# Attention scores in four 32-row strips of the array, values after every key tile, keys split late

## The chip, the cores and the metric

The kernel runs on one core of one Trainium2 chip. The metric is the device time of one execution in microseconds; the time before is the median of three runs, 962.56 us (960.89 to 963.39).

## The reference

The input is one sequence of S = 2048 tokens of width D = 448. Attention with 16 heads of 28 and one shared key and value head is mixed, by a gate per token, with a token-shift MLP:

```python
g = sigmoid((x * gate_w).sum(-1, keepdims=True))
# A: grouped attention, H = 16, Dh = 28, one k and one v for all heads
q = (x @ wq).reshape(B, S, H, Dh).transpose(0, 2, 1, 3)
k, v = x @ wk, x @ wv
scores = einsum("bhqd,bkd->bhqk", q, k) * Dh ** -0.5
a = einsum("bhqk,bkd->bhqd", softmax(scores), v) ... @ wo
# B: layernorm, w1, gelu, four shifted quarters, w2, residual, then an MLP of 1792
h = gelu(layernorm(x) @ w1)
x1 = x + concat(shift(h quarters by +1, -1, +2, -2)) @ w2
b = x1 + gelu(layernorm(x1) @ w3) @ w4
out = g * a + (1 - g) * b
```

All inputs and outputs are fp32.

## The kernel before

Operands that need more precision than one fp32r matmul gives are split into a high part (a rounded copy) and a low part (the rest), and a product is the sum of three: high x high, low x high, high x low.

The kernel writes its instruction order by hand for all engines (`manual_schedule`), so each engine runs its instructions in the order in which the program issues them; waits come from the data. There are three stages.

1. Projections and token shift. `stage_q` projects q, and in spare columns k, v and the gate, for each of the four blocks of 512 tokens and each of four groups of heads, and writes them to DRAM (`qd`). `stage_kv` reads the rows of k back three times into `kf` (rows 0, 32 and 64) and those of v into `vT`, on the SP queue. `split_k` on POOL makes `kS` of it: high keys in rows 0 to 31 and 32 to 63, low keys in rows 64 to 95, ones in rows 96 to 127. It is called for block 0 before `stage_w1(2)`, for block 1 after `stage_w2(1)`, for block 2 after `stage_w1(3)` and for block 3 after `stage_w2(2)`. `kf` has two buffers. `stage_w2(3)` has the splits of the first w3 and w4 chunks between its tiles (`weights`), and these raise a memset of the padded rows on POOL (`split_w_high`, L110) and further loads on SP (`load_w34`, L548 and L549).
2. The MLP, by token block b and by chunk f of 128 of the 1792 columns: `w3_part` (11 matmuls, L134 to L138), two Gelu activations on ACT into `gh` and `gf` (L625, L626), the low part `gl` on DVE (L627), then `w4_part` two chunks later (12 matmuls, L635 to L637). The w3 products alternate between two banks (`mm_tile`).
3. Attention, in 16 units u: a block of 512 queries by a group of four heads. Scores are keys by queries, for 16 key tiles kt of 128 keys and four heads j. The queries of a unit stand in `qs`: high, low and high rows below one another (`q_rows`, three copies of rows on SP a unit), and two rows with the negative maximum, high and low. So one matmul of 98 rows gives all three split products and subtracts the maximum:

```python
nc.tensor.matmul(ps, kS[0:98, kt * P:(kt + 1) * P], q_of[u][0:98, j, :], start=True, stop=True)
```

ACT takes the exponential (L860), and `pv_group` multiplies it with the values and a column of ones, the four heads of a key tile in four column strips of 32 of the array, fp32 (two instructions each). The scores use seven PSUM banks in turn (`bank`); the value sums have one of their own. `VISITS` says after which key tiles PE goes to the values, and for how many of them:

```python
VISITS = {0: (-2, 0), 2: (0, 2), 4: (2, 4), 6: (4, 6), 8: (6, 8), 11: (8, 11), 14: (11, 14)}
```

Seven visits a unit take two or three tiles each. Between the scores, `pump` puts single matmuls of the output projection (`wo_job`, L769 to L773) or, in unit 0, of the last MLP chunk (`w4_job`, L798 to L802), and `max_part` (L210, one 256-column matmul for 64 keys) makes an estimate of the next unit's maxima, which `max_end` sends to rows 96 and 97 of `qs` in four small transfers. After a unit, `sums_begin` copies the value sums (L735), `recip` and `norm` divide (L753), and POOL splits the result (L756, L757) for `wo_job`. If a sum ever grows past a limit, a second pass (`redo`) with exact maxima follows at the end; it is not taken with these inputs.

Of the kernel before, what the change touches and what calls it, by code (L numbers as in the profile page):

```python
# [16 lines left out]
P = 128  # L17
# [24 lines left out]
def gated_mix_kernel(  # L42
# [25 lines left out]
    identR = keep.tile([P, P], F32R, name="identR")  # L68
    nc.vector.tensor_copy(identR, ident)
    x1 = keep.tile([P, NT, D], F32, name="x1")  # L70
    kS = keep.tile([P, S], F32R, name="kS")
# [14 lines left out]
    nc.gpsimd.memset(f32(kS)[96:128, :], 1.0)  # L86
# [53 lines left out]
    def stats_tile(pool, b, t, mv):  # L140
        st = pool.tile([P, 6], F32, tag="st", bufs=4, name=f"st_{pool.name}_{b}_{t}")
        nc.vector.bn_stats(st, x1[:, 4 * b + t, :])
        nc.vector.bn_aggr(mv[:, t, :], st)
# [35 lines left out]
    qs_of = [None, None]  # L179

    def q_load(u, raw):
        b, g = divmod(u, NG)
        qr_of[u] = raw
        nc.sync.dma_start(raw[0:4 * DH], qd[g, 0:4 * DH, 512 * b:512 * b + 512])

    def q_split(u, qh, ql):
        qr = qr_of.pop(u)[0:4 * DH]
        qh_of[u], ql_of[u] = qh[0:4 * DH], ql[0:4 * DH]
        nc.vector.tensor_copy(qh_of[u], qr)
        nc.vector.tensor_sub(ql_of[u], qr, f32(qh_of[u]))  # L190

    def q_rows(u):
        q_of[u] = qs_of[u % 2]
        for r, part in enumerate((qh_of[u], ql_of[u], qh_of[u])):
            nc.sync.dma_start(f32(q_of[u])[32 * r:32 * r + DH], f32(part))

    NU = NB * NG
    q_of = {}
# [7 lines left out]
    def max_part(u, t, tile_of):  # L206
        if t == 0:
            mx_of[u] = late.tile([P, 4, 4], F32, tag="mr", bufs=2, name=f"mr_{u}")
        ps = tile_of(f"m_{u}_{t}")[:, 0:4 * MK].rearrange("p (j k) -> p j k", j=4)
        nc.tensor.matmul(ps, qh_of[u][:, t * P:(t + 1) * P], khd[0:4 * DH], start=True, stop=True)  # L210
        nc.vector.reduce_max(mx_of[u][:, :, t], ps, axis=AX.X)  # L211

    def max_full(u, tile_of):
        mr = late.tile([P, 4, 4], F32, tag="mr", bufs=2, name=f"mf_{u}")
        for j in range(4):
            for t in range(4):
                mk = late.tile([P, NB], F32, tag="mk", bufs=2, name=f"mk_{u}_{j}_{t}")
                for kb in range(NB):
                    ps = tile_of(f"mf_{u}_{j}_{t}_{kb}")
                    nc.tensor.matmul(ps, q_of[u][0:96, j, t * P:(t + 1) * P], kS[0:96, kb * 512:kb * 512 + 512],  # L220
                                     start=True, stop=True)
                    nc.vector.reduce_max(mk[:, kb:kb + 1], ps, axis=AX.X)
                nc.vector.reduce_max(mr[:, j, t:t + 1], mk, axis=AX.X)
        mx_of[u] = mr

    def max_end(u):
        mr = mx_of.pop(u).rearrange("p j t -> p (j t)")
        mc = late.tile([P, 32], F32R, tag="mc", bufs=2, name=f"mc_{u}")
# [3 lines left out]
        mrow = late.tile([P, 32], F32, tag="mrow", bufs=2, name=f"mrow_{u}")  # L232
        nc.vector.transpose(mrow, f32(mc))
        for p in range(4):
            nc.sync.dma_start(f32(qs_of[u % 2])[96:98, :, :].rearrange("k j (t p q) -> k p (j t) q", p=4, q=32)[:, p],
                              mrow[32 * p:32 * p + 32, :])
# [4 lines left out]
    with tc.tile_pool(name="s1b", bufs=1) as s1b, \  # L241
# [77 lines left out]
        kf_of = {}  # L319

        def stage_kv(b):
            cols = slice(512 * b, 512 * b + 512)
            kf = s1b.tile([96, 512], F32, tag="kf", bufs=2, name=f"kf_{b}")
            for r in range(3):
                for g in range(2):
                    nc.sync.dma_start(kf[32 * r + 16 * g:32 * r + 16 * g + 16, :], qd[g, 4 * DH:P, cols])
            for g in range(2):
                nc.sync.dma_start(vT[32 * b + 16 * g:32 * b + 16 * g + 16, :], qd[2 + g, 4 * DH:P, cols])
            kf_of[b] = kf

        def split_k(b):
            cols = slice(512 * b, 512 * b + 512)
            kf = kf_of[b]
            nc.gpsimd.tensor_copy(kS[0:96, cols], kf)
            nc.gpsimd.tensor_tensor(kS[64:96, cols], kf[64:96, :], f32(kS)[64:96, cols], ALU.subtract)
# [172 lines left out]
        split_k(0)  # L508
# [10 lines left out]
        split_k(1)  # L519
# [3 lines left out]
        split_k(2)  # L523
# [3 lines left out]
        late = ctx.enter_context(tc.tile_pool(name="late", bufs=1, side="right", reuse_waits="tile"))  # L527
        khd = late.tile([P, 4, MK], F32R, name="khd")
        qh0 = late.tile([P, 512], F32R, tag="qh0", bufs=1, name="qh0")
        qs_of[0] = late.tile([P, 4, 512], F32R, name="qs0")  # L530
# [70 lines left out]
    with tc.tile_pool(name="s2", bufs=1, reuse_waits="tile") as s2, \  # L601
# [12 lines left out]
        def w3_part(b, f):  # L614
# [3 lines left out]
            if (b, f) == (NB - 1, NF - 1):  # L618
                gh = late.tile([P, 512], F32R, tag="qh0", bufs=1, name="gh_late")
# [4 lines left out]
            gf = s2.tile([P, 512], F32, tag="gf", bufs=2, name=f"gf_{b}_{f}")  # L624
# [14 lines left out]
        for b in range(NB):  # L639
            acc = [ps2.tile([P, 512], F32, tag="acc", bufs=4, name=f"acc_{b}_{t}") for t in range(4)]  # L640
            gs = {}
            for f in range(NF):
# [24 lines left out]
                if b == 1 and f == 1:  # L667
                    for z in (khd, qs_of[0][0:96]):
                        nc.gpsimd.memset(f32(z), 0.0)
                    for j in range(4):  # L670
                        nc.sync.dma_start(f32(khd)[j:4 * DH:4, j, :], f32(kS)[0:DH, 0:MK])
                    q_load(0, s2a.tile([P, 512], F32, tag="xn", bufs=1, name="qr_0"))
                if b == 1 and f == 5:
                    q_split(0, qh0, s2.tile([P, 512], F32R, tag="gl", bufs=3, name="ql_0"))
                    q_rows(0)
# [20 lines left out]
    with tc.tile_pool(name="s3", bufs=1, reuse_waits="tile") as s3, \  # L696
# [12 lines left out]
        qs_of[1] = s3.tile([P, 4, 512], F32R, name="qs1")  # L709
        nc.gpsimd.memset(f32(qs_of[1])[0:96], 0.0)  # L710
# [4 lines left out]
        def q_begin(u):  # L715
            q_split(u, s3.tile([P, 512], F32R, tag="qh", bufs=2, name=f"qh_{u}"),
                    s3.tile([P, 512], F32R, tag="ql", bufs=1, name=f"ql_{u}"))
# [3 lines left out]
        q_rows(1)  # L721
# [40 lines left out]
        def wo_job(u, t, end=None):  # L762
# [4 lines left out]
            held = banks.pop(0)  # L767
            ps = held[:, 0:D]
            nc.tensor.matmul(ps, onh[:, tok], woh[:, g, :], start=True, stop=False)  # L769
            yield  # L770
            nc.tensor.matmul(ps, onh[:, tok], wol[:, g, :], start=False, stop=False)  # L771
            yield
            nc.tensor.matmul(ps, onl[:, tok], woh[:, g, :], start=False, stop=True)  # L773
            banks.append(held)
# [17 lines left out]
        def w4_job(t):  # L792
# [3 lines left out]
            held = banks.pop(0)  # L796
            ps = held[:, 0:D]
            nc.tensor.matmul(ps, gh[:, tok], w4h[-1][:, 1, :], start=True, stop=False)  # L798
            yield
            nc.tensor.matmul(ps, gh[:, tok], w4l[-1][:, 1, :], start=False, stop=False)  # L800
            yield
            nc.tensor.matmul(ps, gl[:, tok], w4h[-1][:, 1, :], start=False, stop=True)  # L802
            banks.append(held)
            nc.vector.scalar_tensor_tensor(x1[:, n, :], ps, gi[:, n:n + 1], x1[:, n, :], op0=ALU.mult, op1=ALU.add)

        jobs = []
        current = [None]

        def pump():
            while current[0] or jobs:  # L810
                if not current[0]:
                    current[0] = jobs.pop(0)
                if next(current[0], True) is None:
                    return
                current[0] = None
                return
# [15 lines left out]
        WO_AT = (33, 36, 37, 40, 43, 44, 48, 50, 52, 53, 54, 55)  # L832
        M_AT = (5, 11, 17, 22)
        M_FIRST = (20, 29, 36, 40)
        W4_AT = (22, 29, 36, 37, 38, 41, 49, 50, 51, 54, 58, 61)
        WO_LAST = (36, 37, 38, 49, 50, 51)
        VISITS = {0: (-2, 0), 2: (0, 2), 4: (2, 4), 6: (4, 6), 8: (6, 8), 11: (8, 11), 14: (11, 14)}

        for k in range(NU * NT + 1):
            u, kt = divmod(k, NT)  # L840
            if k < NU * NT:
                if kt == 8 and 0 < u < NU - 1:
                    q_rows(u + 1)
# [3 lines left out]
                if kt == WO_AT[0] // 4 and u > 0:  # L847
                    for t in range(4):
                        jobs.append(wo_job(u - 1, t))
                if k == 0:  # L850
                    for t in range(4):
                        jobs.append(w4_job(t))
                pump_at = W4_AT if u == 0 else WO_AT if u < NU - 1 else WO_LAST
                p_of[k] = []
                for j in range(4):
                    n, at = 4 * k + j, 4 * kt + j
                    ps = bank(f"s_{n}")
                    nc.tensor.matmul(ps, kS[0:98, kt * P:(kt + 1) * P], q_of[u][0:98, j, :], start=True, stop=True)  # L858
                    p = s3.tile([P, 512], F32, tag="p", bufs=PB, name=f"p_{n}")
                    nc.scalar.activation(p, ps, AF.Exp, scale=SCALE)  # L860
                    p_of[k].append(p)
                    if at in pump_at:
                        pump()
                    if at == 12 and sums:
                        norms.append(recip(*sums.pop()))
                    if at == 27 and norms:
                        norm(*norms.pop())
                    m_at = M_AT if u else M_FIRST
                    if u + 1 < NU and at in m_at:
                        t = m_at.index(at)  # L870
                        max_part(u + 1, t, bank)
                        if t == 3:
                            max_end(u + 1)
            if k == NU * NT:
                while current[0] or jobs:
                    pump()
# [49 lines left out]
        def tail_wo(t):  # L926
            for _ in wo_job(u, t, end):
                pass
# [46 lines left out]
        with tc.If(again > 0, label="redo"):  # L975
            for b in range(NB):
                for g in range(NG):
# [3 lines left out]
                    q_rows(u)  # L981
# [3 lines left out]
                    for kt in range(NT):  # L985
                        for j in range(4):
                            ps = bank(f"s2_{u}_{kt}_{j}")
                            nc.tensor.matmul(ps, kS[0:98, kt * P:(kt + 1) * P], q_of[u][0:98, j, :],
                                             start=True, stop=True)
# [59 lines left out]
```

## Time and profile before

| | |
|---|---|
| runs | 960.89, 962.56, 963.39 us; median 962.56 |
| span of the profiled execution | 960.5 us (its own time is not given beside it) |
| PE busy | 950.6 us, 99% of the span |
| ACT busy | 648.1 us, 67% |
| stage 1, to the first w3 product | to 129.1 us |
| stage 3, first to last attention scores | 402.8 to 944.5 us |
| one unit in the middle of stage 3 | 34.0 us |

Engines are PE (matmul), PEld (weight loads, which overlap PE), DVE (VectorE), ACT (ScalarE), POOL (GpSimd) and SP (which here only issues DMAs). In a row of a group, "out<-in" names the tiles, then come the shapes and the count; behind the bar stand the busy time and the mean of one instruction in ns, and then the idle time of the engine in front of them with what ended it. Matmuls are pipelined, so the mean of one (some 0.4 us) is longer than the distance from one to the next. In a timeline a row is start, length, engine, line and operation, merged over neighbours of one kind; in the chain of waits it is start, length, engine, tile and line. The name of a tile stands without its number: the banks of stage 3 are all "bank".

### The profile page before, as it was taken

How to read it: one execution, taken by the hardware profiler on the slowest of the kernel's cores; microseconds unless marked ns; L12 is line 12 of the kernel's file. 1: busy time of each engine (PE TensorE's matmuls, PEld its weight loads, DVE VectorE, ACT ScalarE, POOL GpSimd, SP SyncE). 2: the span in 40 equal slices, each digit the busy share in tenths (PEclk: the TensorE clock that was granted, in tenths of full speed). 3: DMA queues.
4: the chain of work that ended last, by engine and by line, in shares of the span. 5: the costliest groups of instructions: out<-in, count | busy, mean ns of one | idle time of the engine just before them, and what ended most of it. 6: DMA issues, size and time to landing. Idle time of an engine off the chain costs nothing.

```text
span 960.5 us, 13540 instructions
## 1 busy us (share of the span) xinstructions
PE 950.6 (99%) x5203; PEld 633.0 (66%) x5203; DVE 286.4 (30%) x573; ACT 648.1 (67%) x1266; POOL 112.8 (12%) x136
## 2 busy tenths in 40 slices
PE   9999999999999999999999999999999999999997
PEld 6788888888888888754555555555555555545554
DVE  4664254533432421221222212222122222212112
ACT  5442444322322222499999999999999999999994
POOL 3243400200001420040000000000000000000000
PEclk9999999999999999999999999999999999999999
DMA  9812452111300300021011021011111101210101
GB/s 308 276 42 61 139 164 83 41 53 29 83 1 1 83 1 10 23 56 46 19 48 42 22 78 52 17 36 51 44 59 40 47 18 40 75 49 12 37 13 42
DMA packets 44439, 56.22 MB, mean 59 GB/s; under 512 B 9536, under 2 KB 27664, under 8 KB 44368
## 3 DMA queue, kind: packets, MB, share of 16 engines
q1 hardware_dynamic: 41344, 49.82, 17.7%
q10 hardware_dynamic: 3024, 5.47, 1.6%
q8 instruction: 42, 0.69, 0.3%
q14 instruction: 29, 0.24, 0.1%
HBM read 32.19 MB, written 11.67 MB: 46 GB/s over the span
## 4 chain that ended last, share of the span: by engine, by line
PE 96%; DMA 3%; DVE 0%; SPq 0%; issue 0%
PE bank L858 27%; PE pv L827 24%; PE acc L635 5%; PE acc L637 5%; PE acc L636 5%; PE g L135 4%; PE g L134 4%; PE g L136 4%; DMA w2raw<-in_w_dram 1%; PE hs L421 1%; PE hs L420 1%; PE hs L422 1%; PE bank L773 1%; PE bank L771 1%; PE bank L769 1%; PE g L137 1%
## 5 line engine op out<-in xcount | busy, mean ns | idle before, releaser
L860 ACT ACTIVATE p<-bank 128x512 f32<-128x512 f32 x1024 | 511.4, 642 | 34.3 <-PE bank L858 31.4
L858 PE MATMUL bank<-qs,kS 98*128 98x512 f32 x1024 | 306.0, 408 | 0.0
L858 PEld LDWEIGHTS bank<-qs,kS 98*128 98x128 f32 x1024 | 184.3, 188 | 134.0 <-issue 93.1
L827 PE MATMUL pv<-p,vext 128*32 128x512 f32 x2048 | 243.1, 598 | 0.0
L625 ACT ACTIVATE gh<-g 128x512 fp32r<-128x512 f32 x55 | 32.9, 598 | 182.5 <-PE g L138 182.5
L827 PEld LDWEIGHTS pv<-p,vext 128*32 128x32 f32 x2048 | 58.6, 109 | 116.3 <-issue 108.9
L627 DVE TENSOR_TENSOR gl<-gf,gh 128x512 fp32r<-128x512 f32 x55 | 38.3, 697 | 161.9 <-ACT gf L626 157.6
L635 PE MATMUL acc<-w4h,gh 128*128 128x448 f32 x220 | 79.9, 363 | 0.0
L637 PE MATMUL acc<-w4h,gl 128*128 128x448 f32 x220 | 79.9, 363 | 0.0
L636 PE MATMUL acc<-w4l,gh 128*128 128x448 f32 x220 | 79.7, 362 | 0.0
L781 DVE SCALAR_TENSOR_TENSOR ot<-bank,gg,ot 128x448 f32<-128x448 f32 x44 | 30.0, 684 | 143.3 <-ACT p L860 95.7
L135 PE MATMUL g<-al,w3h 128*128 128x512 f32 x168 | 65.6, 391 | 0.0
L134 PE MATMUL g<-ah,w3h 128*128 128x512 f32 x168 | 65.6, 391 | 0.0
L136 PE MATMUL g<-ah,w3l 128*128 128x512 f32 x168 | 65.6, 391 | 0.0
L756 POOL CAST onh<-on 128x512 fp32r<-128x512 f32 x15 | 9.1, 609 | 472.4 <-DVE on L753 472.4
L211 DVE TENSOR_REDUCE mr<-bank 128x4 f32<-128x256 f32 x60 | 25.6, 427 | 105.5 <-PE bank L210 104.4
L636 PEld LDWEIGHTS acc<-w4l,gh 128*128 128x128 f32 x220 | 41.3, 188 | 4.2
L635 PEld LDWEIGHTS acc<-w4h,gh 128*128 128x128 f32 x220 | 41.3, 188 | 4.1
L637 PEld LDWEIGHTS acc<-w4h,gl 128*128 128x128 f32 x220 | 41.3, 188 | 3.0
L735 DVE COPY o<-pv 128x512 f32<-128x512 f32 x15 | 10.4, 691 | 99.4 <-PE pv L827 99.4
L136 PEld LDWEIGHTS g<-ah,w3l 128*128 128x128 f32 x168 | 31.5, 188 | 6.8
L135 PEld LDWEIGHTS g<-al,w3h 128*128 128x128 f32 x168 | 31.5, 188 | 5.6
(195 smaller groups left out, 971.4 us busy)
## 6 DMA issues: line engine op xcount, KB each, us to landing
qs<-qh SPq DMA_DIRECT2D x32, 224.0 KB
qd<-qf ACTq DMA_DIRECT2D x16, 256.0 KB
rb<-rd SPq DMA_DIRECT2D x15, 256.0 KB
x<-in_x_dram SPq DMA_DIRECT2D x4, 896.0 KB
xd<-xt SPq DMA_DIRECT2D x16, 224.0 KB
w34raw<-in_w_dram SPq DMA_DIRECT2D x7, 512.0 KB
qr<-qd SPq DMA_DIRECT2D x16, 224.0 KB
qs<-ql SPq DMA_DIRECT2D x16, 224.0 KB
```

The source lines that it names most:

```text
L134: nc.tensor.matmul(ps, wh[:, c, :], ah[:, c, :], start=(c == 0), stop=False)
L135: nc.tensor.matmul(ps, wh[:, c, :], al[:, c, :], start=False, stop=False)
L136: nc.tensor.matmul(ps, wl[:, c, :], ah[:, c, :], start=False, stop=False)
L625: nc.scalar.activation(gh, ps, AF.Gelu_apprx_tanh)
L627: nc.vector.tensor_sub(gl, gf, f32(gh))
L635: nc.tensor.matmul(ps, gh[:, tok], w4h[i][:, k, :], start=(f == 0), stop=False)
L636: nc.tensor.matmul(ps, gh[:, tok], w4l[i][:, k, :], start=False, stop=False)
L637: nc.tensor.matmul(ps, gl[:, tok], w4h[i][:, k, :], start=False, stop=(f == stop))
L781: nc.vector.scalar_tensor_tensor(ot_of[n], ps, gg[:, n:n + 1], before, op0=ALU.mult, op1=ALU.add)
L827: nc.tensor.matmul(pv[32 * j:32 * j + 32, :], vext[:, kt, :], ps[j], start=(kt == 0), stop=(kt == NT - 1), tile_position=(0, 32 * j))
L858: nc.tensor.matmul(ps, kS[0:98, kt * P:(kt + 1) * P], q_of[u][0:98, j, :], start=True, stop=True)
L860: nc.scalar.activation(p, ps, AF.Exp, scale=SCALE)
```

## The change

Each head's scores are computed in one strip of 32 rows of the array. `kH` and `kL` hold the high and low keys four times, once in each strip of 32 partitions, with two rows of ones behind the 28 key rows; `qh` and `ql` of a unit hold head j in strip j as they come from DRAM, and the maxima go into rows 28 and 29 of each strip (eight small transfers a unit). A score is three matmuls of 30, 28 and 28 rows, issued in three rounds over the four heads, four banks at a time. `q_rows`, `qs` and its copies are gone. The values follow every key tile, two tiles behind the scores (`LAG`). A projection job is issued whole, after the scores of tiles 8, 10, 12 and 14, a maximum matmul after those of tiles 1, 3, 4 and 5. `kf` is one buffer of 128 partitions, filled by eight transfers a block (`load_k`); the splits of blocks 0 to 3 stand in and behind `stage_w2(2)`, and each load waits for the split before. Some pools get fewer buffers (`gf` one, not two), others more (`qh` and `ql` three).

```diff
+    def score(u, ps, j, keys, first=None, i=None):
+        r = 32 * j
+        for n, (rows, w, a) in enumerate(((first or DH + 2, kH, qh_of[u]), (DH, kL, qh_of[u]), (DH, kH, ql_of[u]))):
+            if i is None or n == i:
+                yield n, rows, w[r:r + rows, keys], a[r:r + rows]
...
     def max_end(u):
...
-        for p in range(4):
-            nc.sync.dma_start(f32(qs_of[u % 2])[96:98, :, :].rearrange("k j (t p q) -> k p (j t) q", p=4, q=32)[:, p],
-                              mrow[32 * p:32 * p + 32, :])
+        for k in range(2):
+            for p in range(4):
+                r = 32 * p + 16 * k
+                nc.sync.dma_start(
+                    f32(qh_of[u])[DH + k:P:32, :].rearrange("j (t p q) -> p j t q", p=4, q=32)[p], mrow[r:r + 16, :])
...
+        kf = s1b.tile([P, 512], F32, name="kf")
+        nc.gpsimd.memset(kf, 1.0)
...
+        def load_k(b):
+            for r in range(4):
+                for g, n in ((0, 16), (1, DH - 16)):
+                    at = 32 * r + 16 * g
+                    nc.sync.dma_start(kf[at:at + n, :], rest(g, n, b))

         def split_k(b):
             cols = slice(512 * b, 512 * b + 512)
-            kf = kf_of[b]
-            nc.gpsimd.tensor_copy(kS[0:96, cols], kf)
-            nc.gpsimd.tensor_tensor(kS[64:96, cols], kf[64:96, :], f32(kS)[64:96, cols], ALU.subtract)
+            nc.gpsimd.tensor_copy(kH[:, cols], kf)
+            nc.gpsimd.tensor_tensor(kL[:, cols], kf, f32(kH)[:, cols], ALU.subtract)
...
         stage_w2(0, third)
         stage_kv(2)
         ln1_tile(3, 3)
-        split_k(0)
...
         xt_write(0, xt4)
-        split_k(1)
         for u in range(12, 16):
             stage_q(u)
         stage_w1(3)
-        split_k(2)
         stage_kv(3)
         s1_stack.close()
...
+        kH = late.tile([P, S], F32R, name="kH")
+        kL = late.tile([P, S], F32R, name="kL")
+        load_k(0)
...
         load_w34(0, s2a)
         xt_read(0, xraw2[0])

         def third(t):
             if t == 0:
                 stage_v()
             elif t > 1:
                 ln_split(0, 2 * t - 4, 2 * t - 2)
+            split_k(t) if t < 2 else None
+            load_k(t + 1) if t < 2 else None

         stage_w2(NB - 2, third)
+        split_k(2)
+        load_k(3)
         split_k(3)
...
-            gf = s2.tile([P, 512], F32, tag="gf", bufs=2, name=f"gf_{b}_{f}")
+            gf = s2.tile([P, 512], F32, tag="gf", bufs=1, name=f"gf_{b}_{f}")
...
-        VISITS = {0: (-2, 0), 2: (0, 2), 4: (2, 4), 6: (4, 6), 8: (6, 8), 11: (8, 11), 14: (11, 14)}
-
-        for k in range(NU * NT + 1):
+        WO_AT = (8, 10, 12, 14)
+        M_AT = (1, 3, 4, 5)
+        M_FIRST = (5, 7, 9, 10)
+        LAG = 2
+
+        for k in range(NU * NT + LAG):
             u, kt = divmod(k, NT)
             if k < NU * NT:
-                if kt == 8 and 0 < u < NU - 1:
-                    q_rows(u + 1)
                 if kt == 13 and u + 2 < NU:
                     q_begin(u + 2)
                     q_fetch(u + 3)
...
+                bs = [bank(f"s_{4 * k + j}") for j in range(4)]
+                for i in range(3):
+                    for j in range(4):
+                        for _, _, w, a in score(u, bs[j], j, slice(kt * P, (kt + 1) * P), i=i):
+                            nc.tensor.matmul(bs[j], w, a, start=(i == 0), stop=(i == 2), tile_position=(32 * j, 0))
                 p_of[k] = []
                 for j in range(4):
-                    n, at = 4 * k + j, 4 * kt + j
-                    ps = bank(f"s_{n}")
-                    nc.tensor.matmul(ps, kS[0:98, kt * P:(kt + 1) * P], q_of[u][0:98, j, :], start=True, stop=True)
-                    p = s3.tile([P, 512], F32, tag="p", bufs=PB, name=f"p_{n}")
-                    nc.scalar.activation(p, ps, AF.Exp, scale=SCALE)
+                    p = s3.tile([P, 512], F32, tag="p", bufs=PB, name=f"p_{4 * k + j}")
+                    nc.scalar.activation(p, bs[j], AF.Exp, scale=SCALE)
                     p_of[k].append(p)
...
+                if kt in WO_AT:
+                    t = WO_AT.index(kt)
+                    if u:
+                        wo_job(u - 1, t)
+                    else:
+                        w4_job(t)
...
-            lo, hi = VISITS.get(kt, (0, 0))
-            for kk in range(u * NT + lo, u * NT + hi):
-                if kk >= 0:
-                    pv_group(kk)
+            if k >= LAG:
+                pv_group(k - LAG)
```

More of the change, by code (lines that the diff above doesn't have):

```diff
@@ L227, in max_end @@
         mr = mx_of.pop(u).rearrange("p j t -> p (j t)")
-        mc = late.tile([P, 32], F32R, tag="mc", bufs=2, name=f"mc_{u}")
+        mc = late.tile([P, 32], F32R, tag="mc", bufs=1, name=f"mc_{u}")
         nc.vector.tensor_scalar(mc[:, 0:16], mr, -1.0, None, op0=ALU.mult)
@@ L618, in w3_part @@
             if (b, f) == (NB - 1, NF - 1):
-                gh = late.tile([P, 512], F32R, tag="qh0", bufs=1, name="gh_late")
+                gh = late.tile([P, 512], F32R, name="gh_late")
                 gl = late.tile([P, 512], F32R, name="gl_late")
@@ L667, in gated_mix_kernel @@
                 if b == 1 and f == 1:
-                    for z in (khd, qs_of[0][0:96]):
-                        nc.gpsimd.memset(f32(z), 0.0)
+                    nc.gpsimd.memset(f32(khd), 0.0)
                     for j in range(4):
-                        nc.sync.dma_start(f32(khd)[j:4 * DH:4, j, :], f32(kS)[0:DH, 0:MK])
+                        nc.sync.dma_start(f32(khd)[32 * j:32 * j + DH, j, :], f32(kH)[0:DH, 0:MK])
                     q_load(0, s2a.tile([P, 512], F32, tag="xn", bufs=1, name="qr_0"))
                 if b == 1 and f == 5:
-                    q_split(0, qh0, s2.tile([P, 512], F32R, tag="gl", bufs=3, name="ql_0"))
-                    q_rows(0)
+                    q_split(0, qh0, ql0)
                 if f >= 2:
@@ L795, in w4_job @@
             gh, gl = last_g
-            held = banks.pop(0)
-            ps = held[:, 0:D]
+            ps = bank(f"job_{n}")[:, 0:D]
             nc.tensor.matmul(ps, gh[:, tok], w4h[-1][:, 1, :], start=True, stop=False)
-            yield
             nc.tensor.matmul(ps, gh[:, tok], w4l[-1][:, 1, :], start=False, stop=False)
-            yield
             nc.tensor.matmul(ps, gl[:, tok], w4h[-1][:, 1, :], start=False, stop=True)
-            banks.append(held)
             nc.vector.scalar_tensor_tensor(x1[:, n, :], ps, gi[:, n:n + 1], x1[:, n, :], op0=ALU.mult, op1=ALU.add)
[L806 to L816, printed above, removed]
         p_of, pv_of, sums, norms = {}, {}, [], []
@@ L864, in gated_mix_kernel @@
[L864 to L876, printed above, removed]
@@ new lines, in gated_mix_kernel @@
+                if kt in WO_AT:
[4 more added lines that the diff above has]
+                        w4_job(t)
+                m_at = M_AT if u else M_FIRST
+                if u + 1 < NU and kt in m_at:
+                    t = m_at.index(kt)
+                    max_part(u + 1, t, bank)
+                    if t == 3:
+                        max_end(u + 1)
+            if k >= LAG:
+                pv_group(k - LAG)
@@ L987, in gated_mix_kernel @@
                             ps = bank(f"s2_{u}_{kt}_{j}")
[L988 to L989 removed]
+                            for n, _, w, a in score(u, ps, j, slice(kt * P, (kt + 1) * P)):
+                                nc.tensor.matmul(ps, w, a, start=(n == 0), stop=(n == 2), tile_position=(32 * j, 0))
                             p = s3.tile([P, 512], F32, tag="p", bufs=PB, name=f"p2_{u}_{kt}_{j}")
```

98 lines of the change are left out of this document (33 added, 65 removed).

## The prediction

> **What bounds the kernel now.** I read the page first: the busy shares of part 1, the clock row of part 2 and the costliest groups of part 5.
>
> ```profile
> span 960.5 us, 13540 instructions
> PE 950.6 (99%) x5203; PEld 633.0 (66%) x5203; DVE 286.4 (30%) x573; ACT 648.1 (67%) x1266; POOL 112.8 (12%) x136
> PEclk9999999999999999999999999999999999999999
> L860 ACT ACTIVATE p<-bank 128x512 f32<-128x512 f32 x1024 | 511.4, 642 | 34.3 <-PE bank L858 31.4
> L858 PE MATMUL bank<-qs,kS 98*128 98x512 f32 x1024 | 306.0, 408 | 0.0
> L858 PEld LDWEIGHTS bank<-qs,kS 98*128 98x128 f32 x1024 | 184.3, 188 | 134.0 <-issue 93.1
> L827 PE MATMUL pv<-p,vext 128*32 128x512 f32 x2048 | 243.1, 598 | 0.0
> ```
>
> PE is busy for 99% of the span at full granted clock, so the time is the length of PE's instruction stream. The score matmuls (L858) and the value matmuls (L827) are its largest groups; both belong to the attention stage, which the change rewrites. The same stage by window, one unit (four heads, 512 queries, 16 key tiles) wide, with span, PE, PEld, DVE, ACT and POOL busy, clock and DMA:
>
> ```profile
> 538.10:572.10 34.00, 34.00 (x209) 17.99 (x208) 7.63 (x17) 31.97 (x65) 1.90 (x2) 1.00 0.21 63
> ```
>
> PE fills its 34.00 us and ACT has 31.97 us of exponentials in them. So the stage is PE's, but ACT is close behind: no saving on PE can bring a unit below about 32.0 us, 2 us less than now, 32 us over 16 units.
>
> What PE's 34 us are made of I take from the chain of waits inside the stage and two rows of the timeline:
>
> ```profile
> 408.38 2.06 PE bank L858 x8
> 410.44 1.86 PE pv L827 x16
> ...
> 422.92 0.39 PE bank L210
> ...
> 425.36 2.71 PE pv L827 x24
> 428.07 0.67 PE bank L858 x2
> ...
> 429.83 0.70 PE bank L858 x3
> ...
> 431.68 0.21 PE bank L800
> ```
> ```profile
> 512.57 0.28 PE L210 MATMUL bank<-khd,qh 112*128 112x256 f32 x1
> 512.69 0.63 PE L858 MATMUL bank<-qs,kS 98*128 98x512 f32 x2
> ```
>
> - A score matmul inside a run costs 0.70/3 = 0.234 us. Two scores right behind a value run cost 0.67, not 0.47: entering the full array from the column strips costs 0.20.
> - A value tile (8 records, four column strips side by side, two passes) costs 2.71 - 1.86 = 0.85 to 0.86; two would be 1.72, the run of 16 takes 1.86, so entering the column strips costs 0.13.
> - So one visit to the values costs s = 0.33, take 0.32. A projection matmul costs 0.205 (L800: 0.21), a maximum matmul 0.12 (from 512.57 to 512.69).
>
> Check: 64 x 0.234 + 16 x 0.86 + 7 visits x 0.32 + 12 x 0.205 + 4 x 0.12 = 15.0 + 13.8 + 2.2 + 2.5 + 0.5 = 34.0. This is the row of the window, so the pieces can be used.
>
> **Scores in strips.** Per key tile, four matmuls of 98 rows become twelve of 28 or 30 rows: three rounds, four strips each. No run here uses row strips, so a round is bounded from both sides: 0.234 if four strips run side by side like one full matmul, 4 x 0.234 = 0.94 if one after another. The nearest rows are the column strips of the values, their weight loads in the timeline:
>
> ```profile
> 500.75 0.13 PEld L827 LDWEIGHTS pv<-p,vext 128*32 128x32 f32 x4 [0.30 <-issue]
> 501.18 0.13 PEld L827 LDWEIGHTS pv<-p,vext 128*32 128x32 f32 x4 [0.30 <-issue]
> ```
>
> Four loads of 0.11 each take 0.13 together, and the next four come 0.43 later, the time of one set of strips: strips load and multiply in parallel and the loads hide under the matmuls. A weight load of 128 columns is 0.188 (L858 PEld), still under 0.234. I take 0.234 a round, 0.70 a tile where four scores cost 0.94: 0.24 x 16 = 3.8 us a unit saved.
>
> **Values after every tile.** Sixteen visits a unit replace seven: 9 x 0.32 = 2.9 us given back, if going between row and column strips costs what going between the full array and column strips does. It could cost nothing; I take the measured price of the nearest switch. On that point the Trainium skill (TensorEngine Tiling (Array Packing), Key Properties) says that a change of the tiling mode drains the array, a change of tile does not. By that rule row and column strips are two modes and the price stays; no run here shows the pair.
>
> **Projection and maximum matmuls.** Now they stand between scores of the same full array and cost no switch. Afterwards each of the 4 projection jobs and 4 maximum matmuls of a unit stands between row strips and column strips and adds one more entry into the full array: 8 x 0.20 = 1.6 us (0 if free).
>
> Unit afterwards: 16 x (0.70 + 0.86 + 0.32) + 12 x 0.205 + 4 x 0.12 + 1.6 = 30.1 + 2.5 + 0.5 + 1.6 = 34.6, against 34.0: **+0.6 a unit, +10 us over 16.** PE remains the bound with ACT 2.6 us behind. The scores now take four of the seven banks at once; the first round of the next tile waits for the first exponential of this one, which is done about 0.6 us after this tile's scores, while PE is in the 0.86 us of values: covered while PE is the later. Only if a unit came near 32 us would that cover be gone.
>
> **Smaller edits in the stage.** The 48 copies of query rows leave SP, and nobody on PE waited for them. The maxima go out in eight transfers, not four, once a unit; so queue time rises by about the 2.71 us of this row, in a unit of 34 us that needs them a third of a unit later:
>
> ```profile
> 551.42 2.71 SPq L235 DMA_DIRECT2D qs<-mrow  x4
> 541.19 0.69 DVE L735 COPY o<-pv 128x512 f32<-128x512 f32 x1 [6.91 <-PE pv L827]
> 551.28 0.65 DVE L753 TENSOR_TENSOR on<-o,rb 128x512 f32<-128x512 f32 x1
> ```
>
> The last values of a unit come a tile later (about 2 us), so the copy at 541.19, its sums and the normalisation at 551.28 move back by that; the first projection, at tile 8 (some 17 us into the unit begun at 538.1), still comes behind the 2 us of splitting on POOL. Cost 0, at most 0.5 a unit, 8 us in all.
>
> **K split late.** Here the change moves POOL and SP work into a place where somebody waits. Before, three of the four key blocks are split while PE projects; each block has own load buffers. Afterwards one buffer `kf` serves four blocks in turn, all four splits come behind the last shift activations on POOL, and the loads stand on SP ahead of the second w3/w4 load (L548). Rows: the tile kf, SP, POOL, ACT and PE there.
>
> ```profile
> L326 SPq DMA_DIRECT2D kf<-qd x24: 302/418/721, 51.6 to 100.9; - x24
> L334 POOL CAST kS<-kf x4: 608/611/613, 71.5 to 115.1; 96x512 fp32r<-96x512 f32 x4
> L335 POOL TENSOR_TENSOR kS<-kf,kS x4: 1280/1296/1323, 72.2 to 115.8; 32x512 fp32r<-32x512 f32 x4
> ```
> ```profile
> 66.59 0.25 SPq L362 DMA_DIRECT2D rsd<-rT  x1
> 67.78 0.30 SPq L367 DMA_DIRECT2D rsb<-rsd  x1
> 96.87 4.47 SPq L326 DMA_DIRECT2D kf<-qd  x6
> 121.36 0.58 SPq L548 DMA_DIRECT2D w34raw<-in_w_dram  x1
> ```
> ```profile
> 112.99 0.11 POOL L413 MEMSET hl<- 112x8 f32 x1
> 117.00 1.06 POOL L110 MEMSET w3h<- 64x256 f32 x4
> ```
> ```profile
> 125.96 0.83 ACT L109 CAST w3h<-w34raw 128x768 fp32r<-128x768 f32 x1 [9.90 <-DMA w34raw<-in_w_dram]
> 127.56 0.95 ACT L555 CAST w4h<-w34raw 128x896 fp32r<-128x896 f32 x1
> 131.84 0.60 ACT L625 ACTIVATE gh<-g 128x512 fp32r<-128x512 f32 x1 [3.34 <-PE g L138]
> 132.34 0.59 ACT L626 ACTIVATE gf<-g 128x512 f32<-128x512 f32 x1
> ```
> ```profile
> 131.19 0.39 PE L137 MATMUL g<-ah,w3h 128*128 128x512 f32 x1
> 134.14 0.39 PE L134 MATMUL g<-ah,w3h 128*128 128x512 f32 x1
> ```
>
> A block costs eight issues of 0.42 (3.3 us), a landing (a small transfer's successor is issued 1.2 us after it; I take 1.2 behind the last issue, up to 3) and a split of 0.61 + 1.30 with gaps (2.0): about 6.5 us. The first split runs from 113.0 to 115.0, so the third ends near 128, the fourth near 134.5. Two things queue behind them:
>
> - POOL: the memset that the first w3 chunk needs (117.00 now) goes to 134.5; PE's L137, now at 131.19, waits for it, 3.5 us.
> - SP: the load issued now at 121.36 goes behind the fourth block's eight issues, to 128 + 3.3 = 131.3; it lands after the same 4.6 us (121.36 to 125.96), at 135.9. ACT's queue holds that split (125.96 to 128.5, 2.5 us) ahead of the first Gelu pair (1.1 us), which frees the bank for PE's third w3 product: 139.5 where 134.14 stands now, 5.4 us.
>
> The two overlap; the later one sets it: **+6 us**, since PE has no slack afterwards to win it back. Bounds: 3 (shorter issues) and 13 (issues of 0.72 as in the row at 96.87). The single `gf` buffer costs nothing: its reader on DVE takes 0.70 (row below), and PE has 23 products of 0.2 us and more between two Gelu pairs.
>
> ```profile
> L627 DVE TENSOR_TENSOR gl<-gf,gh 128x512 fp32r<-128x512 f32 x55 | 38.3, 697 | 161.9 <-ACT gf L626 157.6
> ```
>
> **Sum.** 960.5 + 10 + 6 = 976.5 of span. The page gives no time of its own execution beside the span; the median of the shown runs, 962.56, stands 2.1 above the span. So **979 us**, slower by 1.7%.
>
> **Rivals.**
> - *Switches between strip modes are cheap* (the other side). For: s was never measured for this pair, and it is paid sixteen times. Against: the row above, 0.33 for every visit in this trace. Without switches a unit has 27.9 us on PE, with them 34.6; s and the 0.20 scale together, so s = 0.27 brings the whole change to zero, and below s = 0.20 ACT's 32.0 takes over: 960.5 - 32 + 6 + 2 = 937. Chance 0.15, between 937 and 958.
> - *Strips overlap in part* (issue of forty instructions a tile instead of twenty-four, or writes to four banks at once): a round of 0.30 to 0.47. The 768 rounds then cost +51 to +181: 1030 to 1160. For: nothing here has driven four banks at once; against: the column strips overlap fully. Chance 0.16, two thirds of it below 1045. The Trainium skill (TensorE: Matmul & The Clock Gate, Part 3) reports 3.07 times for four row strips; read as a sustained rate that is 0.305 a round, 1034 us.
> - *Strips run one after another*, so the change does not do what it says: weight loads alone 4 x 0.188 = 0.75 a round, matmuls 0.94: +396 to +540, 1375 to 1520. Against: 0.13 for four loads. Chance 0.11.
> - *Both corrections vanish* (somewhat cheaper switches against the stall, within 0.3% of now): 0.04.
>
> **How the numbers follow.** My forecast has the remaining 0.54; its own range is 968 to 1006 (s from 0.30 to 0.34, so +3 to +17; stall 3 to 13; projection waits 0 to 8; a round up to 0.24, +5). The range 940 to 1045 holds it, the middle, most of the fast rival (0.13) and the lower part of the partial overlap (0.10): 0.81. Faster by over 0.3% (what a measurement here can tell from no change) 0.15, within 0.04, slower 0.81.
>
> **What would show it.** In the new trace: four score weight loads starting together and rounds 0.23 apart (right), or score runs near 0.9 or above 1.2 us a tile (overlap fails); the gap from the last value matmul to the next scores, 0.3 a pair (right) or under 0.2 (fast rival); units of 34.6 us with PE full and ACT at 92% (right), or ACT full at 32 (wrong); L137's successor waiting for POOL and the first Gelu for the w3/w4 load, 5 to 6 us of PE idle near 131 to 140 us (right), or the stage beginning at 403 as now (wrong).

## The result: slower, by twice what was forecast

The changed kernel takes 995.97 us (median of 4 runs, 995.75 to 996.22) against 961.72 for the kernel before: a ratio of 1.0356 (95% interval 1.0341 to 1.0370), +34 us. The forecast was 979, +17, with a range of 940 to 1045: the direction and the range held, and both terms of the sum, attention and late split, were too small. The profiled execution has a span of 994.0 us, 33.5 above that of before, and this is where they lie (starts of PE's matmuls in the two traces):

| stretch | before | after | difference |
|---|---|---|---|
| to the first matmul of the third w3 product | 134.1 | 150.0 | +15.8 |
| from there to the first attention score | 268.7 | 269.8 | +1.1 |
| from there to the last value matmul | 544.5 | 561.3 | +16.7 |
| from there to the end | 13.1 | 13.0 | -0.2 |

The page of the changed kernel, the lines that answer to those shown of before:

```profile
span 994.0 us, 18445 instructions
PE 970.8 (98%) x7251; PEld 562.5 (57%) x7251; DVE 287.1 (29%) x572; ACT 651.9 (66%) x1266; POOL 107.5 (11%) x134
PEclk9999969999999999999999999999999999999999
L832 ACT ACTIVATE p<-bank 128x512 f32<-128x512 f32 x1024 | 515.3, 640 | 47.9 <-PE bank L828 45.6
L828 PE MATMUL bank<-qh,kH 30*128 30x512 f32 x1024 | 133.1, 494 | 0.4 <-ACT p L832 0.4
```

PE is still the bound, with two marks against it that before did not have: one slice of the clock row at 6, and ACT's idle time in front of the exponentials up from 34 to 48 us. A unit of the attention stage, by window (span, PE, PEld, DVE, ACT, POOL):

```profile
525.20:560.16 34.96, 34.96 (x340) 13.32 (x336) 7.75 (x17) 32.23 (x65) 1.89 (x2) 1.00 0.06 18
```

34.96 us where it was 34.0, PE full, ACT at 92%. Inside it, the timeline of PE: a plain tile, and one with a projection job.

```profile
539.28 0.51 PE L828 MATMUL bank<-qh,kH 30*128 30x512 f32 x4
539.62 0.41 PE L828 MATMUL bank<-qh,kL 28*128 28x512 f32 x4
539.85 0.40 PE L828 MATMUL bank<-ql,kH 28*128 28x512 f32 x4
540.18 1.06 PE L808 MATMUL pv<-p,vext 128*32 128x512 f32 x8
541.17 0.50 PE L828 MATMUL bank<-qh,kH 30*128 30x512 f32 x4
...
541.75 0.40 PE L828 MATMUL bank<-ql,kH 28*128 28x512 f32 x4
542.07 0.47 PE L769 MATMUL bank<-woh,onh 128*128 128x448 f32 x1
542.38 0.36 PE L770 MATMUL bank<-wol,onh 128*128 128x448 f32 x1
542.58 0.37 PE L771 MATMUL bank<-woh,onl 128*128 128x448 f32 x1
542.88 1.07 PE L808 MATMUL pv<-p,vext 128*32 128x512 f32 x8
```

Read the starts (a bracket at the end of a row gives the idle time before it and what ended it). Four matmuls of a round go side by side: the second round comes 0.34 after the first (0.23 and an entry), the third 0.23 after the second. From scores to scores is 541.17 - 539.28 = 1.89 us, 1.90 in the mean. The job takes 542.88 - 542.07 = 0.81, where its three matmuls alone are 0.62. The stall of the first stage, in the timelines of PE, POOL, SP and ACT:

```profile
130.24 0.39 PE L132 MATMUL g<-ah,w3l 128*128 128x512 f32 x1
144.25 0.79 PE L133 MATMUL g<-ah,w3h 128*128 128x512 f32 x1 [13.62 <-POOL w3h L106]
144.84 0.63 PE L134 MATMUL g<-ah,w3l 128*128 128x512 f32 x1
145.26 0.63 PE L130 MATMUL g<-ah,w3h 128*128 128x512 f32 x1
145.69 0.63 PE L131 MATMUL g<-al,w3h 128*128 128x512 f32 x1
...
149.96 0.41 PE L130 MATMUL g<-ah,w3h 128*128 128x512 f32 x1
```
```profile
112.97 1.30 POOL L337 TENSOR_TENSOR kL<-kf,kH 128x512 fp32r<-128x512 f32 x1
122.04 0.82 POOL L336 CAST kH<-kf 128x512 fp32r<-128x512 f32 x1 [7.76 <-DMA kf<-qd]
132.34 0.61 POOL L336 CAST kH<-kf 128x512 fp32r<-128x512 f32 x1 [8.05 <-DMA kf<-qd]
141.88 0.61 POOL L336 CAST kH<-kf 128x512 fp32r<-128x512 f32 x1 [7.58 <-DMA kf<-qd]
143.89 1.57 POOL L106 MEMSET w3h<- 64x256 f32 x6
```
```profile
114.30 25.75 SPq L332 DMA_DIRECT2D kf<-qd  x24
140.16 0.61 SPq L550 DMA_DIRECT2D w34raw<-in_w_dram  x1
```
```profile
144.70 0.83 ACT L105 CAST w3h<-w34raw 128x768 fp32r<-128x768 f32 x1 [24.11 <-DMA w34raw<-in_w_dram]
147.62 0.59 ACT L632 ACTIVATE gf<-g 128x512 f32<-128x512 f32 x1
```

The chain is the one forecast: split, load, split, load, with POOL idle for 7.6 to 8.1 us in front of each block after the first; behind it the memset that PE's L133 needs, and behind the last load on SP the w3/w4 load that ACT waits for. PE stands idle for 13.6 us, and only for the memset: ACT is done with the first Gelu pair at 148.21 (147.62 + 0.59), so the bank is free when PE reaches the third w3 product at 149.96, which shows no wait. Behind the idle time PE's matmuls start 0.43 apart instead of 0.23 (145.26 to 145.69) until 149.96. The window over the stretch gives the granted clock, 0.59 in the mean; from 144.3 to 149.5 alone it is 0.50:

```profile
129.00:150.00 21.00, 7.38 (x22) 5.48 (x21) 3.56 (x7) 3.46 (x6) 5.31 (x10) 0.59 0.34 110
```

### The profile page after: what moved, and what is told of

Its sections match the earlier page's. It is cut to its first block, busy times and chain, and to the rows that moved or that the text cites. A ratio compares the mean times of both kernels' runs of the same rounds, so it can differ in the third digit from the quotient of the medians.

```text
span 994.0 us, 18445 instructions
## 1 busy us (share of the span) xinstructions
PE 970.8 (98%) x7251; PEld 562.5 (57%) x7251; DVE 287.1 (29%) x572; ACT 651.9 (66%) x1266; POOL 107.5 (11%) x134
## 4 chain that ended last, share of the span: by engine, by line
PE 94%; DMA 2%; SPq 1%; POOL 1%; DVE 0%; issue 0%; ACT 0%; POOLq 0%; DVEq 0%; ACTq 0%
PE pv L808 25%; PE bank L828 23%; PE acc L642 4%; PE acc L641 4%; PE acc L643 4%; PE g L131 4%; PE g L132 4%; PE g L130 4%; PE bank L769 2%; PE bank L204 2%; SPq L332 1%; PE g L133 1%; PE bank L771 1%; PE g L134 1%; PE bank L770 1%; PE h L130 1%
## 5 line engine op out<-in xcount | busy, mean ns | idle before, releaser
L808 PE MATMUL pv<-p,vext 128*32 128x512 f32 x2048 | 272.9, 604 | 0.0
L828 PEld LDWEIGHTS bank<-qh,kH 30*128 30x128 f32 x1024 | 51.7, 181 | 214.4 <-ACT p L832 212.9
L828 PE MATMUL bank<-qh,kH 30*128 30x512 f32 x1024 | 133.1, 494 | 0.4 <-ACT p L832 0.4
L828 PE MATMUL bank<-qh,kL 28*128 28x512 f32 x1024 | 105.7, 391 | 0.0
L828 PE MATMUL bank<-ql,kH 28*128 28x512 f32 x1024 | 105.6, 388 | 0.0
L808 PEld LDWEIGHTS pv<-p,vext 128*32 128x32 f32 x2048 | 40.6, 108 | 76.5 <-issue 62.8
L828 PEld LDWEIGHTS bank<-ql,kH 28*128 28x128 f32 x1024 | 52.6, 185 | 9.1
L828 PEld LDWEIGHTS bank<-qh,kL 28*128 28x128 f32 x1024 | 51.9, 185 | 0.0
```

What stands on the lines that cost most here:

```text
L808: nc.tensor.matmul(pv[32 * j:32 * j + 32, :], vext[:, kt, :], ps[j], start=(kt == 0), stop=(kt == NT - 1), tile_position=(0, 32 * j))
L828: nc.tensor.matmul(bs[j], w, a, start=(i == 0), stop=(i == 2), tile_position=(32 * j, 0))
```

## The experiments

Nine kernels. Theory A is on the first stage: a serial chain of loads and splits. Theory B: a switch between the array's modes costs what it cost before, 0.33 us for a pair. Theory C: four strips run side by side.

### The late split alone, in the kernel before (b_klate)

```diff
-            kf = s1b.tile([96, 512], F32, tag="kf", bufs=2, name=f"kf_{b}")
+            kf = s1b.tile([96, 512], F32, tag="kf", bufs=1, name=f"kf_{b}")
...
+            split_k(t) if t < 2 else None
+            load_k(t + 1) if t < 2 else None
         stage_w2(NB - 2, third)
+        split_k(2)
+        load_k(3)
         split_k(3)
```

> The kernel before with only the late split: one kf buffer, loads of a block behind the split of the block before, splits in and behind stage_w2(2). Its loads are six transfers of contiguous rows a block. Theory A: issue price decides. With 6 x 0.46 + 1.9 + 2.0 = 6.6 us a block the fourth split ends near 135, PE waits 4 us at the last w3 chunk and 5 to 6 us in all: 967 us. Rival: the delay is that of the changed kernel whatever the form of the transfers, 13 us of waiting and 17 in all: 978 us.

967.60 us (ratio 1.0064, 1.0047 to 1.0080): +6.3, near what the prediction gave for the stall in the changed kernel; 4.6 of it stand at the third w3 product in the trace (138.77 against 134.14). POOL idles 4.2 to 4.4 us for a block and PE 3.0, and here too the clock is half for a while (0.43 apart from 134.87 to 137.0, granted clock 0.50):

```profile
119.12 0.61 POOL L337 CAST kS<-kf 96x512 fp32r<-96x512 f32 x1 [4.20 <-DMA kf<-qd]
125.51 0.85 POOL L337 CAST kS<-kf 96x512 fp32r<-96x512 f32 x1 [4.41 <-DMA kf<-qd]
```
```profile
134.28 0.79 PE L137 MATMUL g<-ah,w3h 128*128 128x512 f32 x1 [3.01 <-POOL w3h L110]
```

So the order of the work alone costs 6 us with loads of 4.3 us. With loads of 7.8 it costs 16: three loads longer by 3.5 are 10.5 us, and PE's idle time grew by 10.6 (3.0 to 13.6).

### One transfer for eight (a_few)

```diff
+            for g, n in ((0, 16), (1, DH - 16)):
+                nc.sync.dma_start(kd[b][16 * g:16 * g + n].rearrange("(j c) s -> j c s", c=4), rest(g, n, b))
...
-            for r in range(4):
-                for g, n in ((0, 16), (1, DH - 16)):
-                    at = 32 * r + 16 * g
-                    nc.sync.dma_start(kf[at:at + n, :], rest(g, n, b))
+            nc.sync.dma_start(kf, kd[b].unsqueeze(0).broadcast_to([4, 32, 512]))
```

> The changed kernel, but each block of keys is first gathered in DRAM (in time that is free on SP), so that the late load of a block is one transfer instead of eight; order of loads, splits and w3/w4 loads as in the changed kernel. Theory A (the first stage's delay is the serial chain of 8 issues of 0.72 us, landing and split, four times): a block costs about 0.7 + 1.9 + 2.0 = 4.7 us instead of 10, the fourth split ends near 128.5, ahead of PE's need at 130.5, and the second w3/w4 load is issued near 124.5. PE does not wait, its clock does not fall, stage 3 begins near 403 us, 979 us in all (16 to 17 below the changed kernel). Rival (splitting late by itself is what costs, whatever the issues cost): at least 6 us of the delay stay, 985 us or more.

989.77 us (ratio to before 1.0297, 1.0280 to 1.0314): only 6 us came back, and the expected 979 was missed. One issue of 0.56 us replaces 5.8 us of issuing, but the transfer of 256 KB lands 4.4 to 6.5 us behind its issue (the waits below less 0.56), not 1.9:

```profile
121.63 0.62 POOL L337 CAST kH<-kf 128x512 fp32r<-128x512 f32 x1 [7.04 <-DMA kf<-kd]
128.60 0.61 POOL L337 CAST kH<-kf 128x512 fp32r<-128x512 f32 x1 [4.91 <-DMA kf<-kd]
136.94 0.61 POOL L337 CAST kH<-kf 128x512 fp32r<-128x512 f32 x1 [6.35 <-DMA kf<-kd]
```

The rival's number (985 or more) came true, its reason did not: the chain is still the cause, and the price of a link is the time from the first issue to the last byte, of which issuing is one part.

### The chain broken (a_kfix)

Keys gathered beforehand as in a_few, four transfers a block, and blocks 2 and 3 behind what PE needs first:

```diff
+            for r in range(4):
+                nc.sync.dma_start(kf[32 * r:32 * r + 32, :], kd[b])
...
-            load_k(t + 1) if t < 2 else None
+            load_k(1) if t < 1 else None
...
-        split_k(2)
-        load_k(3)
-        split_k(3)
...
         stage_w2(NB - 1, weights)
+        load_k(2)
+        split_k(2)
+        load_k(3)
+        split_k(3)
```

> The changed kernel with its first stage's chain broken: keys gathered in DRAM beforehand, a block loaded by four transfers of contiguous rows (4 x 0.42 of issue and 1.5 of landing, as in b_klate, not the 5 to 7 us of the one large transfer in a_few), and blocks 2 and 3 loaded and split behind the w3/w4 loads and memsets that PE needs first. Theory A: stage 3 begins at 403 us, 979 us in all; units stay at 34.96. Rival (something else in the changed first stages costs as well): above 982.

979.02 us (1.0184, 1.0168 to 1.0199). Stage 3 begins at 402.7, units stay at 34.96. The row of L134 in PE's timeline, which waits on that memset, has no wait left:

```profile
129.78 0.39 PE L133 MATMUL g<-ah,w3l 128*128 128x512 f32 x1
130.01 0.39 PE L134 MATMUL g<-ah,w3h 128*128 128x512 f32 x1
130.23 0.39 PE L135 MATMUL g<-ah,w3l 128*128 128x512 f32 x1
```

The first stage thus explains 17 us of the 34, the attention stage the rest.

### Values after every tile, in the kernel before (b_visit16)

```diff
-        VISITS = {0: (-2, 0), 2: (0, 2), 4: (2, 4), 6: (4, 6), 8: (6, 8), 11: (8, 11), 14: (11, 14)}
+        VISITS = {kt: (kt - 2, kt - 1) for kt in range(NT)}
...
+            if k == NU * NT:
+                hi = 0
```

> The kernel before, but PE goes to the values after every key tile, for one tile. Theory B (a visit costs 0.33 us of PE, whoever asks for it): 9 more visits a unit, 9 x 0.33 x 16 = 48 us, 1010 us, unit 37.0 us. Rival (the price was partly a wait for banks or for the exponentials, which shorter visits would ease, as ACT is only busy 94% of a unit): under 30 us, below 992.

1007.95 us (1.0481, 1.0464 to 1.0499), +46.7, units of 36.94: nine visits more are 2.9 us (34.04 before), 0.32 each. Theory B holds for the full array and column strips:

```profile
587.20:624.10 36.90, 36.90 (x210) 16.22 (x209) 7.75 (x17) 33.01 (x64) 1.90 (x2) 1.00 0.12 34
```

### Fewer places for jobs and maxima, in strips (a_kfix_merge)

```diff
-        WO_AT = (8, 10, 12, 14)
-        M_AT = (1, 3, 4, 5)
+        WO_AT = (9, 9, 11, 11)
+        M_AT = (9, 9, 11, 11)
...
```

> As a_kfix, and the four projection jobs and four maximum matmuls of a unit stand in two places (two jobs and two maxima behind the scores of tiles 9 and 11) instead of eight. Theory B (each place costs 0.20 us of entry into the full array): six places fewer, 1.2 us a unit, 19 us in all: 960 us, level with the kernel before, units 33.8. Rival (the jobs hold banks that the next scores need; waits take the place of the entries): units 34.5 or more, 972 or above.

966.46 us (1.0054, 1.0040 to 1.0067): 12.6 us below a_kfix, units of 34.20, between the two numbers. The entries saved are as expected: two jobs behind one another and two maxima take 1.64 us in the trace, where they took 2 x 0.81 + 2 x 0.32 = 2.26 apart. But thirteen plain tiles now follow one another, and after the first five they take 1.95 us instead of 1.90, because the last matmul of the first round waits for its bank. The row of four is 0.56 long instead of 0.51; in the one at 576.07 the fourth matmul starts 0.055 behind the third, where 0.003 is usual:

```profile
574.17 0.51 PE L830 MATMUL bank<-qh,kH 30*128 30x512 f32 x4
...
576.07 0.56 PE L830 MATMUL bank<-qh,kH 30*128 30x512 f32 x4
...
578.03 0.56 PE L830 MATMUL bank<-qh,kH 30*128 30x512 f32 x4
...
579.98 0.57 PE L830 MATMUL bank<-qh,kH 30*128 30x512 f32 x4
```

The starts are 1.90, then 1.96 and 1.95 apart: four exponentials at 0.48 to 0.49. This is the cover that the prediction named as gone near 32 us a unit. It is gone tile by tile, wherever no job gives ACT time to catch up.

### Two rounds of three (a_tworounds)

The third round, low queries by high keys, is left out.

```diff
-                for i in range(3):
+                for i in range(2):
...
-... start=(i == 0), stop=(i == 2), tile_position=(32 * j, 0))
+... start=(i == 0), stop=(i == 1), tile_position=(32 * j, 0))
```

> The changed kernel without the third round (low queries by high keys is left out of the scores). Theory (a round is 0.23 us of PE, and ACT is the next bound with 64 exponentials of 0.48 us, 30.5 us a unit): PE needs 34.96 - 16 x 0.23 = 31.3 a unit, so units of 31.3 to 32.5 and 940 to 956 us. Rival 1 (rounds hide each other, PE's time is in the switches alone): units stay above 34, about 990. Rival 2 (four banks at a time starve ACT once PE is no longer the slower one): units of 33 or more, 965 and above.

949.11 us in a single run, units of 32.07, both inside the first theory's numbers: a round is worth 2.9 us a unit (PE's 3.7 less what ACT takes back), and with PE relieved ACT is nearly full, at the 32.0 us that the prediction named as the floor:

```profile
547.80:579.90 32.10, 32.10 (x276) 10.57 (x272) 7.75 (x17) 31.76 (x66) 1.89 (x2) 1.00 0.14 47
```

### Head by head instead of round by round (a_byhead)

```diff
-                for i in range(3):
-                    for j in range(4):
+                for j in range(4):
+                    for i in range(3):
```

> The changed kernel with the twelve score matmuls of a key tile in another order: the three of one head behind one another, then the next head, instead of three rounds over the heads. Theory C (strips run side by side, matmuls start in program order, those of one strip 0.23 apart): a head's three start 0 / 0.23 / 0.46 and the next head's first starts with the third, so a tile's scores take 4 x 0.46 + 0.23 = 2.1 us instead of 0.70, and the time rises by 1.4 x 256 = 350 us to about 1345. Rival 1 (PE overlaps strips out of order): 0.70 stays, 996 us. Rival 2 (matmuls of strips do not overlap when issued so): 12 x 0.23 = 2.8 us a tile, +530 us, about 1525.

997.74 us in a single run, units of 35.19: rival 1, and the forecast of 1345 was wrong by all of its 350 us. In the instruction stream a head's three matmuls stand together; the trace shows them started in rounds:

```profile
554.68 0.53 PE L828 MATMUL bank<-qh,kH 30*128 30x512 f32 x4
555.02 0.42 PE L828 MATMUL bank<-qh,kL 28*128 28x512 f32 x4
555.25 0.42 PE L828 MATMUL bank<-ql,kH 28*128 28x512 f32 x4
```

Four matmuls of the first kind come ahead of the first one of the second kind. That the stream did change shows in their single starts, 10 ns apart here (554.68 to 554.71) and 3 ns apart with rounds written out. In this trace a strip does not wait for another's matmuls. The order of rounds that the change writes out is worth 0.2 us a unit.

### Fewer visits in the kernel before (b_visit6, b_visit5)

If a visit costs 0.33 us, six or five a unit should beat seven.

```diff
+        VISITS = {0: (-2, 0), 3: (0, 3), 6: (3, 6), 9: (6, 9), 12: (9, 12), 14: (12, 14)}   # b_visit6
+        VISITS = {0: (-3, 0), 3: (0, 3), 6: (3, 6), 9: (6, 9), 13: (9, 13)}                 # b_visit5
```

> The kernel before with six visits to the values a unit instead of seven (five of them, or all but two, of three tiles, twelve scores between). Theory B (0.33 us a visit): one visit fewer, 0.33 x 16 = 5.3 us, 956 us, units of 33.7. Rival (twelve scores in a row run PE ahead of ACT by more than the seven banks hold; the wait eats the gain): 960 us or above, units of 34.0 or more.

> The kernel before with five visits a unit (three of three tiles, one of four after tile 13, three at the head of the next unit). Theory B: two visits fewer, 10.6 us, 951 us, units of 33.4. Rival (banks, as before, and in the visit of four tiles, 3.4 us, ACT runs out of scores after seven banks, 3.3 us): 958 us or above, units of 33.8 or more.

997.19 (1.0379, 1.0359 to 1.0398) and 1011.86 us (1.0518, 1.0504 to 1.0533): slower by 36 and 50, the rival in both. In b_visit6 twelve scores stand between two visits, and the last of them wait for a bank, as the weight loads show:

```profile
586.57 0.28 PE L210 MATMUL bank<-khd,qh 112*128 112x256 f32 x1
586.70 1.97 PE L858 MATMUL bank<-qs,kS 98*128 98x512 f32 x4
588.60 2.78 PE L827 MATMUL pv<-p,vext 128*32 128x512 f32 x24
```
```profile
587.19 0.19 PEld L858 LDWEIGHTS bank<-qs,kS 98*128 98x128 f32 x1 [0.30 <-ACT p L860]
587.68 0.19 PEld L858 LDWEIGHTS bank<-qs,kS 98*128 98x128 f32 x1 [0.30 <-ACT p L860]
```

Four scores take 1.90 us, 0.48 each, the pace of ACT, where 0.23 is PE's. Neither pattern of fewer visits pays with seven banks. No version tried that computes all three products beats the kernel before; a_tworounds (949.11) leaves one out. Strips with fewer visits than sixteen were not run.

## Why the prediction was right, and where its sizes were off

- **PE bounds the stage before and after.** Right: PE fills the unit of 34.96 us, ACT is at 92%, the share named.
- **A round costs 0.234 with four strips side by side.** Right, 0.23 (539.62 to 539.85). The rivals of partial and of no overlap fall. The Trainium skill (TensorE: Matmul & The Clock Gate, Part 3) reports 3.07 times for four row strips; read as a sustained rate, that is an estimate of 0.305 a round, and the trace shows 0.23, four matmuls in the time of one.
- **Row strips and column strips switch at the price of the full array.** Right in kind, a little small: s is 0.34 in the new trace (1.90 - 0.70 - 0.86), taken as 0.32. 0.02 x 16 x 16 is 5 us, and with 34.04 before and 34.96 after a unit grew by 0.92, not 0.6. b_visit16 gives 0.32 for the full array. The rival of cheap switches falls.
- **Jobs and maxima gain an entry of 0.20 each.** Right: a job takes 0.81 (0.615 + 0.20), and merging them saved the entries: two places at 2.26 - 1.64 = 0.62 are 1.24 us a unit, of which 0.76 came through (34.96 to 34.20) and ACT took the rest.
- **The edges of the stage** were not in the sum. With values two tiles behind the scores, the last unit ends later: 35.8 us from its first exponential to the last value matmul, against 33.4. 15 x 0.92 = 13.8, 2.4 for the last unit and 0.6 until the first exponential: together 16.8, where 16.7 was measured and +10 forecast.
- **K split late.** The chain and its two victims were right; the size, and which victim sets it, were not. "Eight issues of 0.42" took the price of contiguous rows. The change also moves the spare columns of `qd`, so that the source rows of a transfer lie in four places 32 rows apart:

```diff
-                    nc.sync.dma_start(kf[32 * r + 16 * g:32 * r + 16 * g + 16, :], qd[g, 4 * DH:P, cols])
...
+            return qd[g].rearrange("(j c) s -> j c s", c=32)[0:n // 4, DH:32, cols]
```

Such transfers take 0.61 to 0.77 each, 5.8 us a block instead of 3.3; the landing is 1.9, not 1.2. A link became 9.9 us, not 6.5 (the first split ends at 114.27, the fourth at 143.83), three links 10.1 longer, and the +3.5 of the POOL path became 13.6 of idle time. The prediction took its +6 from the other path, the w3/w4 load and ACT, as the later one; that path cost nothing that shows, because PE came for the bank only at 149.96. A second step was left out altogether: after 13.6 us of idle PE starts at half clock, and thirteen matmuls take 5.71 us (144.25 to 149.96), where at 0.228 each they would take 2.96: 2.8 us more. 13.6 + 2.8, less the 0.7 by which PE was early (first w3 product at 128.39, not 129.13), is the 15.8 of the table within 0.1. It lies outside the term's own bounds of 3 to 13. The total still fell into the forecast's own 968 to 1006, because that range also allowed 8 us for projection waits and 5 for a slower round, neither of which came. Without them it would have ended near 993, so that much of the hit is luck.

The tile of the loads in the changed kernel shows the mis-sized term (minimum, median and maximum of one issue in ns, to be held against 302/418/721 before). The second row is that of b_klate, where contiguous rows are loaded in the same place:

```profile
L332 SPq DMA_DIRECT2D kf<-qd x32: 607/709/767, 102.0 to 139.3; - x32
L326 SPq DMA_DIRECT2D kf<-qd x24: 303/420/423, 102.5 to 130.0; - x24
```

- **A single `gf` buffer and the copies on SP** show no wait on PE. The MLP stage is 1.1 us longer in the changed kernel, a_few and a_kfix and not in b_klate, in small steps that have no wait behind them. Its cause stays open.

## What to carry to other kernels

Price a moved transfer by its own form, from first issue to last byte, and by the links of the chain it stands in: an error of 0.3 us a transfer became 7 us here because 24 issues stood in series, and 0.7 a landing another 2. Count the entries into another mode of the array as matmuls: here a pair costs 0.32 to 0.34 us, about 1.4 scores. Sixteen pairs instead of seven and eight entries for jobs took back more than the 3.8 us a unit that running four strips at once had saved. Before merging visits or jobs, ask how far PE may run ahead: with seven banks, ACT's 0.48 us an exponential decides as soon as PE has nothing else to do for a tile.

## What the runs showed of the hardware that was not expected

- Row strips ran independently of the order in the instruction stream: head by head and round by round differ by 0.2 us in 35 (a_byhead). The Trainium skill (TensorE: Matmul & The Clock Gate, Part 3) says that matmuls start in program order; in this trace the fourth head's first matmul starts 0.31 us ahead of the first head's second, which stands eight places earlier in the stream.
- One transfer of 256 KB is only 0.6 to 3.2 us quicker than eight of 24 and 32 KB: 4.9 to 7.0 us of POOL's waiting (a_few) against 7.6 to 8.1, although it takes a tenth of the issue time. Its source differs as well (64 KB read four times), so the runs do not say what of this is size.
- A gap of 3.0 us on PE was enough to bring the half clock back for about 2.9 us of work (b_klate, granted clock 0.50, rows 0.43 apart from 134.28 to 137.2); after 8.7 us it lasted 3.6 (a_few), after 13.6 us 5.7 (the changed kernel).
